# Two interleaved attention and GLU layers on one core: block loads of x, larger stores and head-major loads of block 0, and four attention shifts on TensorE

## The chip, the cores and the metric

The kernel runs on one core of one Trainium2 chip. The metric is the device time of one execution in microseconds (us), the median of several runs. Before the change it is 1635.7 us (three runs, 1635.6 to 1635.84).

## The reference

Two rounds of an attention layer and a gated layer over x of 2048 tokens and 1024 features, all in bf16; each layer works on the layer norm of its input and is added to it.

```python
# attention: 32 heads of 32, window of 8 positions at distance 2 (this token and those 2, 4 .. 14 before it)
qkv = x @ wqkv
idx = pos[:, None] - arange(8) * 2            # masked where negative
logits = einsum("bhsd,bhswd->bhsw", q, k[idx]) * 32 ** -0.5
attn = softmax(logits)
o = einsum("bhsw,bhswd->bhsd", attn, v[idx]) @ wo
# gated layer, F = 3584
h = relu(x @ W_gate) * (x @ W_up)
y = h @ W_down
```

## The kernel before, in words

The 2048 tokens are cut into 4 blocks of 512 tokens (`BLK`), and each block into 4 tiles of 128 (`TPB`). The layers are L = 0 and 2 (attention) and L = 1 and 3 (gated). x stays in SBUF for the whole kernel, in 16 tiles of 128 tokens by 1024 features.

The order on every engine is written out by a small planner, `Plan`. Each piece of work is a step with a due time; `plan.run` sorts the steps by time and issues them in that order, and every engine executes its own steps in the order in which they were issued. `on_pe` hands out TensorE's time group by group (0.216 us a matmul of 512 columns) and so sets the pace. VectorE's attention steps form a chain with ready times, and other VectorE steps are put between them. Weight slabs of 1 MB pass through a ring of five buffers. The due times are only estimates: on the chip each step waits for what it needs, and whatever is behind it on the same engine waits as well.

One attention block goes like this:

- `plan_ln` normalises the block: statistics on ScalarE (an Identity and a Square pass with an accumulator, lines 234 and 235) or on VectorE (`bn`, line 223), 1/sqrt on GpSimd (line 256), the normalised tokens by ScalarE into `xn_all` (line 267; one buffer for all blocks), and two DMA transposes from SP into `xnT` (line 273). Block 0 has its own form in which TensorE transposes.
- `plan_proj` makes q, k and v in the order q, k, v: for each, 8 groups of 8 matmuls (line 391), each group into one of the eight PSUM buffers, evicted by ScalarE (`evict`, line 400) into a staging tile. After every second eviction ScalarE issues a store to the DRAM tensors `q_d`, `k_d` or `v_d` (lines 405 and 408), and GpSimd stores the last 14 tokens of k and v again as the halo of the next block.
- `plan_attn` loads q, k and v back head-major: partition 32·tq + h holds head h of token tile tq, with 32 features by 128 tokens (142 with the halo). Each `piece` (line 519) is a DMA from SP that fills 32 partitions, so there are four for each of q, k and v. On VectorE each of the 8 shifts is a product `pr` (`mul`, line 533) and adds and folds over the 32 features (lines 543, 550, 551); then soft-max with `exp` on ScalarE (line 566), and 8 groups of products with v and their adds (lines 584 to 594). Each group's result goes to `o_d` by a DMA from GpSimd (line 595) and comes back by four DMAs as `oT` (`load_o`, line 603).
- `plan_wo` multiplies by wo: 8 groups of 8 matmuls (line 665) and the residual add on VectorE (line 672), after which the next layer norm begins.

Block 0 of layer 0 is special (`first_logits`). q and k stay in SBUF as `q_fm` and `k_fm`, evicted at line 459 and stored in pairs of chunks at lines 465 and 467. The first `NPE` = 3 of its 8 shifts are done feature-major: VectorE multiplies (`prod`, line 487) and TensorE sums over the features with 32 matmuls into `Lps` (line 497). The other 5 are done head-major after the loads. No other block has shifts on TensorE.

The gated layer is `plan_gu` (gate and up, line 695, `relu` on ScalarE at line 702, product `hT` on VectorE at line 710) and `plan_down` (line 741, add at line 749).

Layer 0 runs over all four blocks first: q, k, v of block 0, of block 1 and so on. The output product of block 0, `wo(0, 0)`, is put inside the projections of block 3 by a hook, here after the third group of k:

```python
hooks = {("k", 0, 2): lambda: wo(0, 0)} if L == 0 and b == NB - 1 else {}
```

The gated layer of block 0 follows v of block 3. The DMAs that SP issues go out in one order: loads of x, slabs, head-major loads, oT loads and transposes. A DMA also waits for an earlier one whose completion semaphore it reuses; there are eight of those for SP and ScalarE together.

Of the kernel before, what the change touches and what calls it, by code (L numbers as in the profile page):

```python
# [9 lines left out]
BF16 = mybir.dt.bfloat16  # L10
# [4 lines left out]
P = 128  # L15
D = 1024
H = 32
DH = 32
W = 8
DIL = 2  # L20
HALO = (W - 1) * DIL
KC = D // P
BLK = 512
TPB = BLK // P
# [3 lines left out]
ROW = HALO + BLK  # L28
# [1 line left out]
DG = 4  # L30
RING = 5
NG = DH // DG
NPE = 3


MM = 0.216
# [1 line left out]
T_LAND = 7.0  # L38
PIECE = 4.5


def _ap(t, off, dims):
    return bass.AP(tensor=t.tensor, offset=t.offset + off, ap=[list(t.ap[0])] + [list(d) for d in dims])


def _dram(t, off, dims):
    return bass.AP(tensor=t.tensor, offset=t.offset + off, ap=[list(d) for d in dims])
# [74 lines left out]
def kernel(  # L122
# [11 lines left out]
    nc = tc.nc  # L134
# [3 lines left out]
    NB = S // BLK  # L138
    NT = S // P
# [3 lines left out]
    x_dram = A_x.flatten_outer_dims()  # L143
# [8 lines left out]
    xpool = ctx.enter_context(tc.tile_pool(name="xres", bufs=1))  # L152
# [16 lines left out]
    q_d = [dram.tile([D, BLK], BF16, name=f"q_d{b}") for b in range(NB)]  # L169
    k_d = [dram.tile([D, ROW], BF16, name=f"k_d{b}") for b in range(NB)]  # L170
    v_d = [dram.tile([D, ROW], BF16, name=f"v_d{b}") for b in range(NB)]
    o_d = [dram.tile([TPB, H, DH, P], BF16, name=f"o_d{b}") for b in range(NB)]
    x_tiles = [xpool.tile([P, D], BF16, name=f"x{t}") for t in range(NT)]

    def consts_early():
        nc.gpsimd.memset(ident[:], 1.0)
# [26 lines left out]
    plan = Plan(RING)  # L203
# [243 lines left out]
    def first_logits(st, tm):  # L447
        hold = {}

        def begin():  # L450
            hold["q"] = tpose.tile([P, KC * BLK], BF16, tag="T", name="q_fm")
            hold["k"] = tpose.tile([P, FRONT + KC * BLK], BF16, tag="T", name="k_fm")
            nc.gpsimd.memset(hold["k"][:, 0:FRONT], 0.0)

        def evict(nm, c, acc, t):
            def f():
                f0 = FRONT if nm == "k" else 0
                fm = hold[nm]
                nc.scalar.copy(fm[:, f0 + c * BLK:f0 + (c + 1) * BLK], acc()[:])
                if c % 2 == 0:  # L460
                    return
                src = fm[:, f0 + (c - 1) * BLK:f0 + (c + 1) * BLK].rearrange("p (c n) -> p c n", c=2)
                r0 = (c - 1) * P
                if nm == "q":
                    nc.scalar.dma_start(_dram(q_d[0], r0 * BLK, [[BLK, P], [P * BLK, 2], [1, BLK]]), src)
                    return
                nc.scalar.dma_start(_dram(k_d[0], r0 * ROW + HALO, [[ROW, P], [P * ROW, 2], [1, BLK]]), src)
                nc.gpsimd.dma_start(_dram(k_d[1], r0 * ROW, [[ROW, P], [P * ROW, 2], [1, HALO]]), src[:, :, BLK - HALO:BLK])
            if nm == "q" and c == 0:
                plan.at(t - 1.0, begin)  # L470
            plan.at(t, f)
            if nm == "k":
                plan.chain.append((lambda: t + 0.7, 1.2, mul(c), None))

        def mul(c):
            def f():
                if c == 0:
                    pr = held[:, 3 * KC:3 * KC + NPE, :]
                elif c == 1:
                    pr = at_pool.tile([P, NPE, BLK], BF16, tag="l1", name="prod_1")  # L480
                else:
                    if c == 2:
                        hold["pr"] = hm_pool.tile([P, 2, NPE, BLK], BF16, tag="v", name="prod_2")
                    elif c % 2 == 0:
                        hold["pr"] = at_pool.tile([P, 2, NPE, BLK], BF16, tag="pr", name=f"prod_{c}", bufs=2)
                    pr = hold["pr"][:, c % 2]
                nc.vector.tensor_tensor(pr[:], _ap(hold["q"], c * BLK, [[0, NPE], [1, BLK]]),
                                        _ap(hold["k"], FRONT + c * BLK, [[-DIL, NPE], [1, BLK]]), op=ALU.mult)
                hold[("pr", c)] = pr
            return f  # L490

        def red():
            L = hold["L"] = psum.tile([P, NPE, P], F32, tag="acc", name="Lps")
            for c in range(KC):
                pr = hold.pop(("pr", c))
                for tq in range(TPB):
                    nc.tensor.matmul(L[32 * tq:32 * tq + 32, :, :], lhsT=wide[:, 28 - 4 * c:60 - 4 * c],
                                     rhs=pr[:, :, tq * P:(tq + 1) * P], start=(c == 0), stop=(c == KC - 1),
                                     skip_group_check=True, tile_position=(0, 32 * tq))

        def out():
            st["L"] = at_pool.tile([P, W, P], F32, tag="L", name="L_0_0")
            nc.scalar.copy(st["L"][:, 0:NPE, :], hold["L"][:])

        def step():
            plan.at(plan.on_pe(8.0, red) + T_EV, out)

        return {"evict": evict, ("v", 0, 3): step}


    def plan_attn(L, b, ends, st, tm):

        def load(t, parts, gap=PIECE):

            def piece(nm, src, row, n, tq):
                def f():
                    if tq == 0:
                        st[nm] = hm_pool.tile([P, DH, n], BF16, tag=nm, name=f"{nm}hm_{L}_{b}")
                    nc.sync.dma_start(st[nm][32 * tq:32 * tq + 32, :, :],
                                      _dram(src[b], tq * P, [[DH * row, H], [row, DH], [1, n]]))  # L520
                return f
            for p in parts:
                for tq in range(TPB):
                    plan.at(t, piece(*p, tq))
                    t += gap
            return t - gap + T_LAND
# [81 lines left out]
        prev = list(chain_tm)  # L608
        chain_tm.append(tm)

        def qk_ready():
            if first:
                load(ends["q"] + 5.5, (("q", q_d, BLK, P),), 1.5)
                tm["qk_in"] = load(ends["k"] + 4.0, (("k", k_d, ROW, HALO + P),), 1.5)
                return tm["qk_in"]
            t = max(ends["k"] + 6.0, prev[-1]["logits"] + 0.5)
            tm["qk_in"] = load(t, (("q", q_d, BLK, P), ("k", k_d, ROW, HALO + P)))
            return tm["qk_in"]

        def v_ready():  # L620
            t = max(ends["v"] + 6.0, tm["qk_in"] + 10.0)
            if prev:
                t = max(t, prev[-1]["pv"] + 0.5)
            return load(t, (("v", v_d, ROW, HALO + P),))

        now = lambda: 0.0
        first = L == 0 and b == 0
# [146 lines left out]
    def proj(L, b):  # L774
        st, tm = {}, {}
        if L == 0 and b == 0:
            hooks = first_logits(st, tm)
        else:
            hooks = {("k", 0, 2): lambda: wo(0, 0)} if L == 0 and b == NB - 1 else {}
        attn[(L, b)] = plan_attn(L, b, plan_proj(L, b, hooks), st, tm)  # L780

    def wo(L, b):
        plan_wo(L, b, attn[(L, b)], plan_ln(L + 1, b))

    def late_ln(L, b, t, on_vector=False):
        for i, f in enumerate(plan_ln(L, b, on_vector=on_vector)):
            f(t + 2.7 * i * (not on_vector))


    def load_x(t, eng=nc.sync):  # L790
        return lambda: eng.dma_start(x_tiles[t][:], x_dram[t * P:(t + 1) * P, :])  # L791
# [16 lines left out]
    for t, at in ((1, -6.7), (2, -6.3), (3, -6.2)):  # L808
        plan.at(at, load_x(t))
    plan.at(14.0, consts_late)  # L810
    for b in range(1, NB):
        for t in range(b * TPB, (b + 1) * TPB):
            plan.at((-4.5, -1.5, 20.5)[b - 1], load_x(t))

    for b in range(NB):
        if b == 0:
            late_ln(0, 1, plan.pe + 7.0, on_vector=True)
            late_ln(0, 2, plan.pe + 30.0)
        elif b == 1:
            late_ln(0, 3, plan.pe + 15.0)  # L820
        proj(0, b)
    for b in range(NB):
        if b >= 1:
            late_ln(2, b - 1, plan.pe + 30.0)
        glu[b] = plan_gu(1, b)
        if b + 1 < NB:
            wo(0, b + 1)
        else:
            wo(2, 0)
        plan_down(1, b, glu[b], False)  # L830
        if b >= 1:
            if b == NB - 1:
                late_ln(2, b, plan.pe + 15.0)
            proj(2, b - 1)
    for b in range(NB):
        glu[b] = plan_gu(3, b)
        if b == 0:
            proj(2, NB - 1)
        if b + 1 < NB:
            wo(2, b + 1)  # L840
        plan_down(3, b, glu[b], True)
# [35 lines left out]
```

## Time and profile before

| | |
|---|---|
| median of three runs | 1635.7 us |
| profiled execution, its own time | 1636.91 us |
| its span, first to last instruction | 1635.2 us |
| TensorE busy | 1617.6 us, 99% of the span |
| VectorE busy | 1045.1 us, 64% |
| ScalarE busy | 448.6 us, 27% |
| GpSimd busy | 102.5 us, 6% |
| mean granted TensorE clock | 0.997 |
| DMA | 319 MB in 456298 packets, mean 195 GB/s |

Times in the profile count from the first instruction of the span. "PE" is TensorE, "PEld" its weight loads, "DVE" VectorE, "ACT" ScalarE, "POOL" GpSimd and "SP" the sync engine, which issues most DMAs; a "q" behind an engine's name is its instruction queue. `xnT<-xn_all` is a DMA or an instruction that writes `xnT` from `xn_all`. The waits of an engine read: who waited at which line, for what, us in total, how often, and the longest.

### The profile page before, as it was taken

How to read it: one execution, taken by the hardware profiler on the slowest of the kernel's cores; microseconds unless marked ns; L12 is line 12 of the kernel's file. 1: busy time of each engine (PE TensorE's matmuls, PEld its weight loads, DVE VectorE, ACT ScalarE, POOL GpSimd, SP SyncE). 2: the span in 40 equal slices, each digit the busy share in tenths (PEclk: the TensorE clock that was granted, in tenths of full speed). 3: DMA queues.
4: the chain of work that ended last, by engine and by line, in shares of the span. 5: the costliest groups of instructions: out<-in, count | busy, mean ns of one | idle time of the engine just before them, and what ended most of it. 6: DMA issues, size and time to landing. Idle time of an engine off the chain costs nothing.

```text
span 1635.2 us, 19283 instructions
## 1 busy us (share of the span) xinstructions
PE 1617.6 (99%) x7658; PEld 741.1 (45%) x7658; DVE 1045.1 (64%) x1297; ACT 448.6 (27%) x718; POOL 102.5 (6%) x170
## 2 busy tenths in 40 slices
PE   9999899999999999999999999999999999999999
PEld 5444344444444444444444444444444444444444
DVE  5399979999999449880598706996999211211211
ACT  4662411303230342403413151133011301121110
POOL 2122000000000100001000010000000000000000
PEclk9999999999999999999999999999999999999999
DMA  9986868778956889568795699599846755565442
GB/s 294 188 212 155 190 162 215 190 192 201 244 168 205 242 192 232 157 212 246 192 228 170 209 228 217 162 265 237 224 149 198 197 176 160 175 173 162 155 164 68
DMA packets 456298, 319.13 MB, mean 195 GB/s; under 512 B 204016, under 2 KB 452240, under 8 KB 456208
## 3 DMA queue, kind: packets, MB, share of 16 engines
q1 hardware_dynamic: 424992, 283.60, 66.1%
q10 hardware_dynamic: 26544, 25.50, 5.3%
q0 software_dynamic: 4672, 8.80, 1.8%
q8 instruction: 60, 0.98, 0.3%
q14 instruction: 30, 0.25, 0.1%
HBM read 263.98 MB, written 38.15 MB: 185 GB/s over the span
## 4 chain that ended last, share of the span: by engine, by line
PE 92%; DMA 3%; DVE 2%; SPq 1%; ACT 1%; issue 0%; ACTq 0%; DVEq 0%
PE acc_g L695 24%; PE acc_u L695 24%; PE dacc L741 24%; PE acc_wo L665 6%; PE acc_k L391 5%; PE acc_q L391 5%; PE acc_v L391 5%; DMA xnT<-xn_all 1%; DVE l L543 1%; SPq L791 1%; DMA x<-in_A_x_dram 1%; DVE pr L533 1%; DMA oT<-o_d 1%; DMA k_d<-stage_k 0%; SPq L198 0%
## 5 line engine op out<-in xcount | busy, mean ns | idle before, releaser
L695 PE MATMUL acc_g<-xnT,wg 128*128 128x512 bf16 x1792 | 425.0, 380 | 6.6 <-DMA xnT<-xn_all 6.6
L695 PE MATMUL acc_u<-xnT,wu 128*128 128x512 bf16 x1792 | 424.5, 380 | 0.0
L741 PE MATMUL dacc<-wd,hT 128*128 128x512 bf16 (+1 forms) x1820 | 388.1, 376 | 0.0
L710 DVE TENSOR_TENSOR hT<-acc_u,r 128x512 bf16<-128x512 f32 x224 | 154.2, 689 | 326.7 <-PE acc_u L695 321.4
L702 ACT ACTIVATE r<-acc_g 128x512 bf16<-128x512 f32 x224 | 133.6, 596 | 710.0 <-PE acc_g L695 710.0
L695 PEld LDWEIGHTS <-wg 128*128 128x128 bf16 x1792 | 175.6, 98 | 219.2 <-issue 8.7
L741 PEld LDWEIGHTS <-hT 128*128 128x128 bf16 x1820 | 178.1, 98 | 209.0
L695 PEld LDWEIGHTS <-wu 128*128 128x128 bf16 x1792 | 175.7, 98 | 212.7 <-issue 2.2
L533 DVE TENSOR_TENSOR pr<-qhm,khm 128x4096 bf16<-128x4096 bf16 x61 | 139.3, 2283 | 24.3 <-DMA khm<-k_d 24.3
L543 DVE TENSOR_TENSOR l<-l,pr 128x1024 f32<-128x1024 f32 x122 | 149.0, 1221 | 2.7
L584 DVE TENSOR_TENSOR pvt<-a,vhm 128x4096 bf16<-128x4096 bf16 x64 | 146.2, 2284 | 0.2
L749 DVE TENSOR_TENSOR x<-dacc,x 128x512 bf16<-128x512 f32 (+1 forms) x65 | 42.9, 680 | 123.4 <-PE dacc L741 123.1
L665 PE MATMUL acc_wo<-wo,oT 128*128 128x512 bf16 x512 | 112.2, 379 | 2.8 <-DMA oT<-o_d 2.8
L391 PE MATMUL acc_v<-xnT,wv 128*128 128x512 bf16 x384 | 84.5, 379 | 0.4 <-ACT stage_k L400 0.3
L391 PE MATMUL acc_q<-xnT,wq 128*128 128x512 bf16 x384 | 84.2, 379 | 0.0
L391 PE MATMUL acc_k<-xnT,wk 128*128 128x512 bf16 x384 | 84.2, 379 | 0.0
L234 ACT ACTIVATE xn_all<-x 128x1024 bf16<-128x1024 bf16 x56 | 59.0, 1053 | 81.4 <-DVE x L672 72.6
L592 DVE TENSOR_TENSOR pvt<-pvt 128x2048 bf16<-128x2048 bf16 x64 | 78.1, 1221 | 1.4
L665 PEld LDWEIGHTS <-oT 128*128 128x128 bf16 x512 | 49.8, 98 | 64.0 <-DMA oT<-o_d 4.3
L267 ACT ACTIVATE xn_all<-x,nb,rstd 128x1024 bf16<-128x1024 bf16 x60 | 72.0, 1234 | 18.9 <-DVE nb L261 15.1
L595 POOL DMA_DIRECT2D o_d<-ohm x64 | 35.3, 552 | 644.3 <-DVE ohm L594 630.7
L543 DVE TENSOR_TENSOR l<-pr 128x1024 f32<-128x1024 bf16 x61 | 74.3, 1218 | 0.8
(84 smaller groups left out, 826.2 us busy)
## 6 DMA issues: line engine op xcount, KB each, us to landing
wg<-in_B_W_gate_dram SPq DMA_DIRECT2D x56, 1024.0 KB, 7.0
wu<-in_B_W_up_dram SPq DMA_DIRECT2D x56, 1024.0 KB, 5.3
wd<-in_B_W_down_dram SPq DMA_DIRECT2D x48, 1024.0 KB, 6.4
wo<-in_A_wo_dram SPq DMA_DIRECT2D x16, 1024.0 KB, 7.0
wq<-in_A_wqkv_dram SPq DMA_DIRECT2D x9, 1024.0 KB, 4.9
wk<-in_A_wqkv_dram SPq DMA_DIRECT2D x9, 1024.0 KB, 5.5
wv<-in_A_wqkv_dram SPq DMA_DIRECT2D x9, 1024.0 KB, 6.0
khm<-k_d SPq DMA_DIRECT2D x32, 284.0 KB, 8.8
```

The lines of the kernel that those rows point to most:

```text
L234: nc.scalar.activation(junk, xt[:], ACT.Identity, accum_out=st[:, 0, t % 2:t % 2 + 1])
L267: nc.scalar.activation(hold["xn"][:, t, :], x_tiles[b * TPB + t][:], ACT.Identity, scale=rstd[:, i:i + 1], bias=nb[:, i:i + 1])
L391: nc.tensor.matmul(acc[:, t0 * P:t1 * P], lhsT=w["t"][:, kc, j * P:(j + 1) * P], rhs=xnT[(L, b)][:, t0:t1, kc, :], start=(kc == 0), stop=( ...
L533: nc.vector.tensor_tensor(pr[:], st["q"][:], _ap(st["k"], HALO - DIL * w, [[HALO + P, DH], [1, P]]), op=ALU.mult)
L543: nc.vector.tensor_tensor(l[:], pr[:, 0:8] if i == 0 else l[:], pr[:, 8 * i + 8:8 * i + 16], op=ALU.add)
L584: nc.vector.tensor_tensor(tt[:], a_bc, v_sh, op=ALU.mult)
L592: nc.vector.tensor_tensor(tt[:, 0:4], tt[:, 0:4], tt[:, 4:8], op=ALU.add)
L665: nc.tensor.matmul(acc[:], lhsT=st["oT"][:, c, t, :], rhs=ws[half]["t"][:, c, :], start=(c == 0), stop=(c == KC - 1))
L695: nc.tensor.matmul(acc[:], lhsT=w["t"][:, kc, (j % 4) * P:(j % 4 + 1) * P], rhs=xnT[(L, b)][:, :, kc, :], start=(kc == 0), stop=(kc == KC ...
L702: nc.scalar.activation(r[:], hold.pop(("g", j))[:], ACT.Relu)
L710: nc.vector.tensor_tensor(st["hT"][:, j, :], hold.pop(("u", j))[:], hold.pop(("r", j))[:], op=ALU.mult)
L741: nc.tensor.matmul(accs[(t, c0)][:], lhsT=st["hT"][:, j, t * P:(t + 1) * P], rhs=w["t"][:, jl, c0 - half * SLAB:c0 - half * SLAB + n], sta ...
```

## The change

It has these parts:

- `NPE` goes from 3 to 4: block 0 of layer 0 has four shifts on TensorE and four on VectorE.
- x is held in one tile a block. Blocks 1, 2 and 3 are loaded by one DMA of 1 MB each, not four of 256 KB; the due time of block 3's load goes from 20.5 to 50.0.
- The stores of `q_fm` take four chunks each (two DMAs, not four); those of `k_fm` take four, two and two (three DMAs).
- The head-major loads of q and k of block 0 of layer 0 take two token tiles each (`m=2`), so two DMAs of 64 partitions stand in place of four of 32, and its v loads are due 2.5 apart.
- The head-major loads of v of block 1 of layer 0 are due after the `oT` loads of block 0.
- The statistics of block 2 of layer 0 are computed on VectorE (`bn`), due at 32 in place of 30 after the start of block 0's projections; those of block 3 are due at 20 in place of 15.
- `wo(0, 0)` is put after the last group of q of block 3, three groups of k sooner.

```diff
-NPE = 3
+NPE = 4
...
-    x_tiles = [xpool.tile([P, D], BF16, name=f"x{t}") for t in range(NT)]
+    x_blk = [xpool.tile([P, TPB, D], BF16, name=f"xb{b}") for b in range(NB)]
+    x_tiles = [x_blk[t // TPB][:, t % TPB, :] for t in range(NT)]
...
-                if c % 2 == 0:
+                n = {3: 4, 5: 2 * (nm == "k"), 7: 2 if nm == "k" else 4}.get(c, 0)
+                if n == 0:
                     return
-                src = fm[:, f0 + (c - 1) * BLK:f0 + (c + 1) * BLK].rearrange("p (c n) -> p c n", c=2)
-                r0 = (c - 1) * P
+                src = fm[:, f0 + (c + 1 - n) * BLK:f0 + (c + 1) * BLK].rearrange("p (c n) -> p c n", c=n)
+                r0 = (c + 1 - n) * P
...
-        def load(t, parts, gap=PIECE):
+        def load(t, parts, gap=PIECE, m=1):
...
-                    nc.sync.dma_start(st[nm][32 * tq:32 * tq + 32, :, :],
-                                      _dram(src[b], tq * P, [[DH * row, H], [row, DH], [1, n]]))
+                    dims = [[DH * row, H], [row, DH], [1, n]]
+                    nc.sync.dma_start(st[nm][32 * tq:32 * (tq + m), :, :],
+                                      _dram(src[b], tq * P, dims if m == 1 else [[P, m]] + dims))
                 return f
             for p in parts:
-                for tq in range(TPB):
+                for tq in range(0, TPB, m):
...
-                load(ends["q"] + 5.5, (("q", q_d, BLK, P),), 1.5)
-                tm["qk_in"] = load(ends["k"] + 4.0, (("k", k_d, ROW, HALO + P),), 1.5)
+                load(ends["q"] + 5.5, (("q", q_d, BLK, P),), 2.0, 2)
+                tm["qk_in"] = load(ends["k"] + 4.0, (("k", k_d, ROW, HALO + P),), 2.0, 2)
...
-            if prev:
-                t = max(t, prev[-1]["pv"] + 0.5)
+            if first:
+                return load(t, (("v", v_d, ROW, HALO + P),), 2.5)
+            t = max(t, prev[-1]["done"] - T_LAND + 1.0 if b == 1 and L == 0 else prev[-1]["pv"] + 0.5)
...
-            hooks = {("k", 0, 2): lambda: wo(0, 0)} if L == 0 and b == NB - 1 else {}
+            hooks = {("q", 1, 3): lambda: wo(0, 0)} if L == 0 and b == NB - 1 else {}
...
-    for b in range(1, NB):
-        for t in range(b * TPB, (b + 1) * TPB):
-            plan.at((-4.5, -1.5, 20.5)[b - 1], load_x(t))
+    for b, at in ((1, -4.5), (2, -1.5), (3, 50.0)):
+        plan.at(at, lambda b=b: nc.sync.dma_start(x_blk[b][:], _dram(x_dram, b * BLK * D, [[D, P], [P * D, TPB], [1, D]])))
...
-            late_ln(0, 2, plan.pe + 30.0)
+            late_ln(0, 2, plan.pe + 32.0, on_vector=True)
         elif b == 1:
-            late_ln(0, 3, plan.pe + 15.0)
+            late_ln(0, 3, plan.pe + 20.0)
```

In the head-major loads the source pattern of a 32-partition load is (rows one `row` apart, 1024 of them; n tokens each); that of a 64-partition load is (2 token tiles, 128 tokens apart; 1024 rows; n tokens). The destinations are 32 and 64 partitions.

More of the change, by code (lines that the diff above doesn't have):

```diff
@@ L459, in f @@
                 nc.scalar.copy(fm[:, f0 + c * BLK:f0 + (c + 1) * BLK], acc()[:])
-                if c % 2 == 0:
+                n = {3: 4, 5: 2 * (nm == "k"), 7: 2 if nm == "k" else 4}.get(c, 0)
+                if n == 0:
                     return
-                src = fm[:, f0 + (c - 1) * BLK:f0 + (c + 1) * BLK].rearrange("p (c n) -> p c n", c=2)
-                r0 = (c - 1) * P
+                src = fm[:, f0 + (c + 1 - n) * BLK:f0 + (c + 1) * BLK].rearrange("p (c n) -> p c n", c=n)
+                r0 = (c + 1 - n) * P
                 if nm == "q":
-                    nc.scalar.dma_start(_dram(q_d[0], r0 * BLK, [[BLK, P], [P * BLK, 2], [1, BLK]]), src)
+                    nc.scalar.dma_start(_dram(q_d[0], r0 * BLK, [[BLK, P], [P * BLK, n], [1, BLK]]), src)
                     return
-                nc.scalar.dma_start(_dram(k_d[0], r0 * ROW + HALO, [[ROW, P], [P * ROW, 2], [1, BLK]]), src)
-                nc.gpsimd.dma_start(_dram(k_d[1], r0 * ROW, [[ROW, P], [P * ROW, 2], [1, HALO]]), src[:, :, BLK - HALO:BLK])
+                nc.scalar.dma_start(_dram(k_d[0], r0 * ROW + HALO, [[ROW, P], [P * ROW, n], [1, BLK]]), src)
+                nc.gpsimd.dma_start(_dram(k_d[1], r0 * ROW, [[ROW, P], [P * ROW, n], [1, HALO]]), src[:, :, BLK - HALO:BLK])
             if nm == "q" and c == 0:
```

## The prediction

> **What bounds the kernel now.** I read the page's busy line first, then the windows by stage, TensorE's waits, the chain, and the DMA part. From the page:
>
> ```profile
> PE 1617.6 (99%) x7658; PEld 741.1 (45%) x7658; DVE 1045.1 (64%) x1297; ACT 448.6 (27%) x718; POOL 102.5 (6%) x170
> ```
>
> TensorE sets the time; only what it loses can be won. The windows (start and end, PE busy, PEld, DVE, ACT, POOL, granted clock, DMA share, GB/s) show where it loses:
>
> ```profile
> 80.00:90.00 10.00, 8.96 (x41) 3.80 (x39) 9.72 (x11) 9.03 (x18) 1.45 (x2) 1.00 1.19 287
> 90.00:100.00 10.00, 9.38 (x42) 4.00 (x41) 9.48 (x19) 7.37 (x12) 3.99 (x4) 1.00 0.90 168
> 100.00:110.00 10.00, 9.24 (x43) 4.12 (x43) 9.62 (x13) 4.78 (x8) 2.90 (x4) 1.00 0.85 198
> 160.00:170.00 10.00, 8.54 (x40) 3.74 (x39) 9.76 (x11) 0.41 (x1) 0.00 (x0) 1.00 1.22 244
> 170.00:180.00 10.00, 8.69 (x41) 3.73 (x39) 9.93 (x14) 6.13 (x11) 0.00 (x0) 1.00 0.75 159
> 200.00:210.00 10.00, 4.03 (x10) 1.46 (x11) 6.72 (x7) 1.50 (x3) 0.00 (x0) 0.58 0.97 241
> 210.00:220.00 10.00, 10.00 (x43) 4.31 (x42) 6.98 (x8) 1.37 (x3) 0.00 (x0) 0.91 0.00 0
> ```
>
> Three places, all in layer 0. TensorE's waits name them:
>
> ```profile
> PE acc_g L695 <- DMA xnT<-xn_all: 6.6, 1, 6.6
> PE acc_wo L665 <- DMA oT<-o_d: 2.8, 2, 1.5
> PE acc_v L391 <- ACT stage_k L400: 1.1, 2, 0.8
> PE acc_q L391 <- ACT stage_v L400: 1.0, 2, 0.7
> ```
>
> and the chain (start, duration, what) shows where each begins:
>
> ```profile
> 34.95 9.09 DMA xnT<-xn_all
> 60.54 2.27 DMA v_d<-stage_v
> 63.41 5.19 DMA khm<-k_d
> 68.77 2.31 DVE pr L533
> ...
> 113.16 13.81 PE acc_k L391 x64
> ...
> 164.88 8.38 DMA oT<-o_d
> 173.31 3.63 PE acc_wo L665 x16
> ...
> 192.50 13.34 DMA xnT<-xn_all
> 205.97 3.57 PE acc_g L695 x8
> ```
>
> A projection of one block takes TensorE 13.81 us. In the timeline k, v and q of blocks 1 and 2 run from 68.03 to 113.00, 44.97 for 3 × 13.81 = 41.43: 3.5 lost. wo of block 0 runs 159.84 to 176.77, 16.93 for 13.81: 3.1. The gate matmuls start at 205.97, though v of block 3 ended at 199.2: 6.8; the clock is then granted at 0.58 and their first 16 take 6.31 for 3.45: 2.9. Together 16.3 us. All hang on VectorE's pass over block 0, which starts only at 68.77, when the last head-major k load lands.
>
> **The change part by part.** Sums stand against the profiled execution's own 1636.9 us (span 1635.2), 1.2 above the median of 1635.7.
>
> *Four shifts on TensorE.* The 32 Lps matmuls ran 45.75 to 47.30 at 384 columns; at 512 they take 4/3 of 1.55: +0.5. VectorE loses one of block 0's five shifts in the first layer, 7.49 (pr 2.28, three adds of 1.22, folds 1.15 and 0.29, less overlap); no other block has shifts on TensorE. The products grow by a third (0.96 to 1.28 each), done before its loads land.
>
> *Stores, loads of x, statistics.* Of k's four stores the third could be issued only at 44.12, when the transposes of block 1 had landed (44.04), and the evictions behind it stood. Fewer, larger q and k stores take away that wait; k's last store goes out near 39.6 instead of 45.63 and lands, at the same 6.4 us, near 46. Block 3's four x loads (issued 39.19 to 41.18) leave their place ahead of the q loads for one behind block 2's transposes; the first q load then issues near 39.2, not 41.28. Nothing reads that x before 72. Block 2's statistics leave ScalarE (four pairs of 2.36) for VectorE (eight of 0.68), which idles from 44 to 68; cost nothing, and if that cover is gone, 5.4 us of VectorE. With them off ScalarE, its 6.57 us wait for the xn_all buffer (72.7 to 79.25), which made the stage_k and stage_v rows above, comes later and with slack.
>
> *wo of block 0 three groups sooner.* It comes 3 × 8 × 0.216 = 5.2 us nearer to the oT loads; good only if VectorE is at least that much earlier. The v loads of block 1 now queue on SP behind the oT loads and no longer among them (oT landings were 159.79, 164.87, 165.70 and 173.26), and both transposes after wo are issued before the 1 MB wu slab that stood between them (issues 188.69, 190.68 and 192.50).
>
> *The head-major loads of block 0* are what I could not price from one row. Two q and two k loads replace four and four; each fills 64 partitions in 64 × 32 = 2048 pieces of 256 or 284 bytes. The piece price is in the trace: two k loads of 1024 pieces issued at 121.43 and 122.01 landed at 126.39 and 127.68, 1.29 us apart, which is 1024/16 = 64 pieces on each of 16 DMA engines and so 20.2 ns a piece. The page's mean is the dear end:
>
> ```profile
> q1 hardware_dynamic: 424992, 283.60, 66.1%
> ```
>
> 1635.2 × 16 × 0.661 / 424992 = 40.7 ns. What the trace cannot show is over how many engines the new form runs. Every transfer before has 32 or more as its outermost count on both sides (a 32-partition load reads 1024 rows one step apart). The new source is [2, 1024, n], the 2 being the pair of token tiles, a step that joins no other. One end: 16 engines, as the nearest rows. Other end: transfers are dealt out by their outermost count, and 2 engines carry 1024 pieces each. I take 2: the outermost count is the one thing in which the form leaves all rows that show 16, and the transfer is addressed in that order. As the four loads are alike, I put them on the same pair.
>
> The Trainium skill has a rule for it: "DMA: Bandwidth & Descriptors", section "Why a DMA increments its semaphore by 16 and not by 1", says that the engines used are the largest number up to 16 dividing the slowest non-unit dimension of both patterns, and for this issuing path the lowest-numbered ones; its "Rules for kernel authors" warn of an outermost dimension under 16. By it all four loads share one pair of engines; the same page's advice to coalesce into larger transfers would give the 16-engine sum. No run so far shows either.
>
> *The sum with 16 engines.* k loads issue near 46; the first pair of 284 KB takes 4.5 + 1.3, the second 2.6 more: VectorE starts near 55, 14 earlier. Four shifts and soft-max (46.8 before, less 7.49: 39.3), and pv (8 × 4.65): block 0 is done near 131.5, not 152.7. oT lands near 150 for a wo at 151.5; the adds end near 174, the transposes land 188 to 191 for gate matmuls at 193. All 16.3 goes, less 0.5: 1636.9 − 15.8 = 1621.1, at the median 1619.9.
>
> *The sum with one pair.* First pieces move 1.3 us after the issue at 39.2, at 40.5. Four loads in line: 4 × 1024 × 20.2 ns = 82.7, so the last lands near 124 and VectorE starts 69 later than with 16. Behind them on the same two engines lie the shares of block 2's transposes and block 3's x. ScalarE's statistics of block 3 stand in the middle of k of block 1's evictions and wait for both; the eight PSUM buffers fill and TensorE stops near 86 until about 130. It then runs 13.8 us to the third group of q of block 2 (at 99.7 undisturbed), whose buffer needs an eviction queued behind exp of block 0. exp starts four shifts and the maxima after VectorE's start, 124 + 4 × 7.49 + 3.8 = 157.8; exp, one normalisation and one eviction (1.06 + 1.24 + 0.57) free the buffer at about 161. TensorE is 161 − 99.7 = 61 late. The stop before it is inside this 61. Restart at the low clock: 2.9. Later wo, adds and transposes hang on VectorE, now 69 late against TensorE's 64, and the slack there is 2 to 4: 1.5 more. 1621.1 + 61.3 + 2.9 + 1.5 = 1686.8, at the median 1685.6.
>
> Bounds: at 40.7 ns the loads take 166.7 and the end is 84 later, 1770; half way (30.4 ns) 1728. If q and k loads fell on different pairs, k would land at 47.3 + 41.4 = 88.7 and the time would be 1650.
>
> **The rivals.** (1) *Loads at full width.* For: all 96 head-major loads before run at some 20 ns over 16 engines, and the bytes are the same. Against: no row with so small an outermost count. Time 1620, faster by 16. It decides from the point where VectorE starts block 0 by 63: then exp frees the buffer before 99.7. (2) *Full width, but the transposes after wo are late again:* four loads of oT and two 512 KB transposes meet slabs of 1 MB; if the second lands 5 us after 193, 5 + 2.9 come back: 1628. (3) *The loads fall on two pairs:* 1650.
>
> **How the numbers follow.** One pair 0.62, two pairs or something between 0.08, full width 0.30 (of which late transposes 0.06). The likeliest gives the predicted 1686; its own range is 1664 (15 ns a piece, an estimate a quarter under the row) to 1735 (30.4 ns and some waits more). As cases of both signs hold most of the chance, the range runs from 1617 to 1735: full width is in it, and what is left out is the dearest part of the pair case. A measurement of this kernel tells about 0.2% (3.3 us) from no change. Faster takes full width, 0.29; within 0.2% 0.01, a late wo that eats just the gain; slower 0.70.
>
> **What would show it.** Right: khm loads of block 0 landing past 100 with first pr after them; DMA share low while they run (2 of 16 engines busy is 0.12 plus the rest); TensorE idle tens of us between 80 and 165, waiting for ScalarE evictions behind statistics of block 3 and exp; a clock below 1 after it; block 1 and later unchanged in shape. Full width: k loads land by 56, first pr near 55, no PE idle at 80 to 110, none or little at wo and at the first gate matmuls. Wrong altogether: VectorE starting early and TensorE still losing time at wo, or a stop where neither sum has one, as at block 2's transposes with all loads landed.

## The result, and the profile after

The changed kernel takes 1688.9 us (median of four, 1688.3 to 1694.8) against 1635.8: 3.3% slower, ratio 1.0332 (95% interval 1.0309 to 1.0355). The prediction said 1686. The profiled execution took 1688.66, its span 1686.9.

The windows after (columns as before):

```profile
80.00:90.00 10.00, 7.99 (x38) 3.50 (x36) 0.00 (x0) 0.00 (x0) 0.00 (x0) 1.00 0.16 30
90.00:100.00 10.00, 0.00 (x0) 0.00 (x0) 0.00 (x0) 0.00 (x0) 0.00 (x0) 0.56 0.17 26
...
140.00:150.00 10.00, 9.35 (x32) 3.73 (x32) 9.72 (x10) 8.53 (x18) 1.45 (x2) 0.71 1.24 261
150.00:160.00 10.00, 3.71 (x18) 1.57 (x16) 9.55 (x15) 1.35 (x3) 1.06 (x2) 0.80 0.38 116
160.00:170.00 10.00, 7.59 (x26) 2.85 (x26) 8.62 (x18) 8.00 (x10) 2.82 (x4) 0.69 0.45 99
```

From 88 to 129 TensorE, VectorE, ScalarE and GpSimd all stand, and from 90 to 120 the DMA engines move some 30 GB/s. The waits of the engines name the chain:

```profile
DVE pr L536 <- DMA khm<-k_d: 95.9, 3, 80.6
...
ACT xn_all L235 <- DMA xb<-in_A_x_dram: 63.0, 1, 63.0
PE acc_v L392 <- ACT stage_k L401: 52.7, 1, 52.7
...
ACT xn_all L268 <- DVE nb L262: 24.2, 14, 8.9
...
PE acc_q L392 <- ACT stage_v L401: 8.7, 2, 8.3
```

VectorE waits 80.6 us for the head-major k loads; ScalarE 63.0 for block 3's x, which is behind those loads on SP; TensorE 52.7 for the evictions behind ScalarE's wait, and 8.3 more later. The chain (start, duration, what) starts the first `pr` at 129.49 where it was 68.77:

```profile
86.44 42.85 DMA khm<-k_d
129.49 2.30 DVE pr L536
```

SP's own timeline shows the four loads:

```profile
42.41 24.55 SPq L522 DMA_DIRECT2D qhm<-q_d  x2
67.15 40.75 SPq L522 DMA_DIRECT2D khm<-k_d  x2
108.02 23.16 SPq L274 DMA_TRANSPOSE xnT<-xn_all  x2
131.23 0.99 SPq L816 DMA_DIRECT2D xb<-in_A_x_dram  x1
```

Before, eight such issues took from 41.28 to 64.07, 0.5 to 2.4 us each. Now the issues end at 43.06, 66.96, 86.39 and 107.90 and the first transpose's at 129.12: SP can go on only once in about 20 us. The DMA view of 90 to 120 has nothing but these pieces in it:

```profile
DMA packets 2972, 0.84 MB, mean 28 GB/s; under 512 B 2972, under 2 KB 2972, under 8 KB 2972
q1 hardware_dynamic: 2972, 0.84, 16.9%
```

If two engines carry them, 2972 pieces in 30 us are 30000 × 2 / 2972 = 20.2 ns a piece and engine, the price that the prediction took from two k loads of the kernel before.

### The profile page after: what moved, and what is told of

Read it like the earlier page. It is cut to its first block, busy times and chain, and to the rows that moved or that the text cites. A ratio compares the mean times of both kernels' runs of the same rounds, so it can differ in the third digit from the quotient of the medians.

```text
span 1686.9 us, 19239 instructions
## 1 busy us (share of the span) xinstructions
PE 1618.1 (96%) x7658; PEld 741.4 (44%) x7658; DVE 1043.9 (62%) x1296; ACT 441.1 (26%) x702; POOL 102.7 (6%) x169
## 4 chain that ended last, share of the span: by engine, by line
PE 86%; DVE 7%; DMA 4%; issue 2%; SPq 0%; POOL 0%; ACT 0%; ACTq 0%; DVEq 0%; POOLq 0%
PE acc_g L699 23%; PE acc_u L699 23%; PE dacc L745 23%; PE acc_wo L669 6%; PE acc_k L392 4%; PE acc_q L392 4%; PE acc_v L392 4%; DMA khm<-k_d 3%; DVE l L546 2%; DVE pr L536 1%; DVE pvt L587 1%; DVE l L553 1%; DVE pvt L595 1%; DMA xnT<-xn_all 0%; SPq L522 0%
## 5 line engine op out<-in xcount | busy, mean ns | idle before, releaser
L753 DVE TENSOR_TENSOR xb<-dacc,xb 128x512 bf16<-128x512 f32 (+1 forms) x65 | 43.3, 681 | 124.4 <-PE dacc L745 124.2
L235 ACT ACTIVATE xn_all<-xb 128x1024 bf16<-128x1024 bf16 x52 | 54.8, 1053 | 136.3 <-DVE xb L676 70.9
L392 PEld LDWEIGHTS <-wqk 128*128 128x128 bf16 x480 | 42.7, 99 | 107.9 <-issue 67.6
L392 PE MATMUL acc_v<-xnT,wqk 128*128 128x512 bf16 x128 | 30.1, 394 | 52.7 <-ACT stage_k L401 52.7
L268 ACT ACTIVATE xn_all<-xb,nb,rstd 128x1024 bf16<-128x1024 bf16 x60 | 71.9, 1233 | 26.9 <-DVE nb L262 24.2
L401 ACT CAST stage_q<-acc_q 128x512 bf16<-128x512 f32 x56 | 32.2, 586 | 170.5 <-PE acc_q L392 162.0
```

What stands on the lines that cost most here:

```text
L235: nc.scalar.activation(junk, xt[:], ACT.Identity, accum_out=st[:, 0, t % 2:t % 2 + 1])
L268: nc.scalar.activation(hold["xn"][:, t, :], x_tiles[b * TPB + t][:], ACT.Identity, scale=rstd[:, i:i + 1], bias=nb[:, i:i + 1])
L392: nc.tensor.matmul(acc[:, t0 * P:t1 * P], lhsT=w["t"][:, kc, j * P:(j + 1) * P], rhs=xnT[(L, b)][:, t0:t1, kc, :], start=(kc == 0), stop=( ...
```

## The experiments

All were timed beside the kernel before on the same chip; its median there was 1637.4 (for the first four runs), 1635.6 (m1_npe3, m1_pairs, head_major_store, m1_stats) and 1635.5 us (the rest). Ratios are to it, with 95% intervals.

**Which property of the loads costs**

*after_m1*: the loads alone put back.

```diff
-                load(ends["q"] + 5.5, (("q", q_d, BLK, P),), 2.0, 2)
-                tm["qk_in"] = load(ends["k"] + 4.0, (("k", k_d, ROW, HALO + P),), 2.0, 2)
+                load(ends["q"] + 5.5, (("q", q_d, BLK, P),), 2.0 / 3)
+                tm["qk_in"] = load(ends["k"] + 4.0, (("k", k_d, ROW, HALO + P),), 2.0 / 3)
```

> The changed kernel with only the head-major q and k loads of block 0 put back to eight DMAs of 32 partitions (outermost count 1024), in the same places. Theory, the four loads ran on two of the 16 engines and that is the whole loss: the last k load lands near 55, the first pr starts near 56 and not 129.5, TensorE loses under 1 us between 80 and 215, and the time is 1619.9 (within 3). Rival, other parts of the change cost as well (a transpose or a wo that is late again): 1625 to 1640. Rival, the loads had nothing to do with it: 1689.

1629.1, ratio 0.9950 (0.9937 to 0.9964); profiled 1629.55. The loads are the loss, but the time is over the stated 1619.9 (within 3): the rest brings 8 us and not 16, as the first rival said. The last k load landed at 65.9 and the first `pr` started at 66.05, not near 56. TensorE's waits:

```profile
PE acc_q L392 <- ACT stage_v L401: 3.1, 3, 2.1
PE acc_k L392 <- DVE xb L676: 3.0, 1, 3.0
PE acc_g L699 <- DMA xnT<-xn_all: 1.8, 1, 1.8
```

*after_rows*: the same 64 partitions and 2048 pieces, another outermost count (the new line is for `m == 2` alone).

```diff
-                                      _dram(src[b], tq * P, dims if m == 1 else [[P, m]] + dims))
+                                          _dram(src[b], min(tq * P, row // 2 - n), [[row // 2, 2 * D], [1, n]]))
```

> The changed kernel with its four loads of 64 partitions and 2048 pieces kept, but each reads 2048 half rows one step apart, so that the outermost count is 2048 and not 2. The pieces have the same size and number; the data are other parts of q and k, so the attention of block 0 in layer 0 is another. Theory, the outermost count alone decides: first pr near 56, 1620 (within 3), like eight loads of 32 partitions. Rival, a DMA of 64 partitions or 2048 pieces is itself slow: first pr near 129 and 1689.

1625.6, ratio 0.9928 (0.9914 to 0.9941), profiled 1623.70; first `pr` at 64.11. That is like after_m1, and not the stated 1620 (within 3). The size of the load is not what costs; in SP's timeline the four issues are short again:

```profile
39.33 8.65 SPq L523 DMA_DIRECT2D qhm<-q_d  x2
52.29 4.83 SPq L523 DMA_DIRECT2D khm<-k_d  x2
```

*after_m4*: one load of 128 partitions for q and one for k.

```diff
-                load(ends["q"] + 5.5, (("q", q_d, BLK, P),), 2.0, 2)
+                load(ends["q"] + 5.5, (("q", q_d, BLK, P),), 2.0, 4)
```

(and k alike)

> The changed kernel with one q and one k load of 128 partitions each, outermost count 4. Theory, as many engines as the outermost count: 2 x 4096 pieces on 4 engines is 2048 each, at 20.9 ns 43 us; the first load issues near 42.4, pieces move from 43.7, the first pr starts near 87, and the third group of q of block 2 gets its buffer near 124 for 99.7: 24 late, restart 2.9, and 1 to 2 later, 1648 in all (1642 to 1654). Rival, two engines whatever the count: 1689. Rival, a larger DMA is quicker: 1620.

1656.8, ratio 1.0120 (1.0105 to 1.0134), profiled 1653.5: between the two, where only "as many engines as the outermost count" puts it, though above the stated 1642 to 1654. First `pr` at 91.70, not 87. TensorE waited 30.6 in place of 24, and not where expected: the wait ends at 95.86, in q of block 1. On ScalarE block 2's normalisation stood ahead of the last evictions of block 0's v and waited for `nb`, which VectorE computed right after the first `pr`:

```profile
94.09 1.24 ACT L268 ACTIVATE xn_all<-xb,nb,rstd 128x1024 bf16<-128x1024 bf16 x1 [41.82 <-DVE nb L262]
```

The DMA view of 70 to 88:

```profile
q1 hardware_dynamic: 3267, 0.93, 33.3%
```

That is twice the share of the loads with a count of 2. On four engines it is 18000 × 4 / 3267 = 22.0 ns a piece.

*before_m2*: the kernel before with only the new loads.

```diff
-                load(ends["q"] + 5.5, (("q", q_d, BLK, P),), 1.5)
+                load(ends["q"] + 5.5, (("q", q_d, BLK, P),), 2.0, 2)
```

(k alike, and `load` and `piece` as in the change)

> The kernel before with only the four loads of 64 partitions (outermost count 2) in place of eight of 32. Theory, this part alone makes the loss: the first q load issues near 41.3, pieces move for 4096 x 20.9 ns = 86 us, the first pr starts near 129 and not 68.8, 60 later; TensorE is later by that less the few us of slack in front of exp: 1690 to 1698. Rival, the loss needs the other parts (moved stores, statistics, wo): under 1680.

1688.3, ratio 1.0314 (1.0300 to 1.0328), 2 under the stated range; first `pr` at 126.44. This one part makes all of the loss; on top of it the rest of the change brings nothing that shows. Here too the stop is not the one in front of `exp`: ScalarE waited 58.6 for `nb`, again behind the first `pr`, and TensorE 56.8 for the evictions behind it.

```profile
ACT xn_all L267 <- DVE nb L261: 77.9, 15, 58.6
...
PE acc_q L391 <- ACT stage_v L400: 62.1, 2, 56.8
```

**Where the other half of the gain went: one part of after_m1 undone at a time**

*m1_npe3*, `-NPE = 4` `+NPE = 3`:

> after_m1 with three shifts on TensorE again. Theory, VectorE's pass over block 0 sets the end of the loss: one shift more is 7.5 us later at exp, wo and the gate matmuls, less 0.5 for Lps and less whatever wait is covered: 5 to 9 slower than after_m1. Rival, the slack covers it: the time of after_m1 within 1.

Ratio 0.9941 (0.9927 to 0.9954): nothing is lost, and the theory fell. One shift more on VectorE, after a first `pr` that is 1.1 later, makes soft-max of block 0 8.7 us later (first `pvt` at 113.96 for 105.26). But the planner then puts the wo adds behind two shifts of block 1 and not three, and they start at 166.13 instead of 170.89.

*m1_pairs*:

```diff
-                n = {3: 4, 5: 2 * (nm == "k"), 7: 2 if nm == "k" else 4}.get(c, 0)
+                n = 2 * (c % 2)
```

> after_m1 with the q_fm and k_fm stores in pairs of chunks again. In after_m1 the second q store took 16 us to land (27.2 to 43.2), and the q loads waited for it. Theory A (the prediction's): pairs bring the third k store's wait for the transposes back, k lands 3 to 6 later: 2 to 6 slower than after_m1. Theory B, the larger stores gain nothing here, as the q loads wait for the last q store: within 2 of after_m1, or faster.

Ratio 0.9950 (0.9938 to 0.9963): theory B in the time, though not in its reason. The last q store landed sooner than in after_m1, at 40.7 for 43.2, but the q loads then waited until 43.3 for the transposes of block 1. The last k store lands at 53.4 instead of 49.8, but the first `pr` moves only from 66.05 to 66.90.

*head_major_store*: q and k stores write the order of the head-major loads.

```diff
-                    nc.scalar.dma_start(_dram(q_d[0], r0 * BLK, [[BLK, P], [P * BLK, n], [1, BLK]]), src)
+                    nc.scalar.dma_start(_dram(q_e, r0 * TPB * P, [[P, P], [P * P, n * TPB], [1, P]]),
+                                        _ap(fm, (c + 1 - n) * BLK, [[P, n * TPB], [1, P]]))
...
+                        nc.sync.dma_start(st[nm][32 * tq:32 * tq + 32, :, :].rearrange("p d n -> p (d n)"),
+                                          _dram(src, tq * P * n, [[TPB * P * n, KC], [DH * n, 4], [1, DH * n]]))
```

> after_m1 with the stores of q and k of block 0 writing DRAM in the order the head-major loads want: the stores have pieces of 256 and 284 bytes (2048 in one of four chunks), the eight loads 32 pieces of 8 or 9 KB each (outermost counts 8 and 32). In after_m1 the eight loads were issued over 43.2 to 60.6 and landed 52.3 to 65.9. Theory A, these loads then land one fast after the other, the last near 56, first pr near 56 and not 66; the 10 us take out the waits at wo and the gate matmuls: 5 to 8 less than after_m1. Theory B, the small pieces only move to the stores, whose landings slip by as much: first pr 63 to 66 and the time of after_m1 within 2.

Ratio 0.9952 (0.9939 to 0.9964): theory B in the time. The last two k stores landed at 57.9 and 59.0, not 49.8, and the first `pr` started at 69.06, later than both theories said.

*m1_stats*:

```diff
-            late_ln(0, 2, plan.pe + 32.0, on_vector=True)
+            late_ln(0, 2, plan.pe + 30.0)
-            late_ln(0, 3, plan.pe + 20.0)
+            late_ln(0, 3, plan.pe + 15.0)
```

> after_m1 with block 2's statistics on ScalarE again (due 30) and block 3's due at 15. Theory (the prediction's), ScalarE's wait for the xn_all buffer returns in the middle of k and v of block 1, and with it some 3.5 us of TensorE between 80 and 110, part of which the later waits would have cost anyway: 1 to 4 slower than after_m1. Rival, with VectorE's start at 66 the end of the layer is set by VectorE alone: within 1.

Ratio 0.9970 (0.9959 to 0.9982), 3 us slower than after_m1. The size was as expected, the place was not: TensorE's largest wait is 4.8 for the wo adds.

*m1_x*: x by tiles, block 3's at 20.5.

```diff
-    for b, at in ((1, -4.5), (2, -1.5), (3, 50.0)):
-        plan.at(at, lambda b=b: nc.sync.dma_start(x_blk[b][:], ...
+    for b in range(1, NB):
+        for t in range(b * TPB, (b + 1) * TPB):
+            plan.at((-4.5, -1.5, 20.5)[b - 1], load_x(t))
```

> after_m1 with x of blocks 1 to 3 loaded by tiles again, block 3's at the old due time, ahead of the q loads. Prediction's theory, the four loads ahead of q delay it by 2 us and so the first pr: 1 to 3 slower than after_m1. Rival, the q loads wait for the q store anyway (43.2): within 1.

Ratio 0.9965 (0.9952 to 0.9977), 2.5 us slower, with the first `pr` at 69.81, 3.8 later. Block 3's four loads do stand at 43.52 to 45.52 ahead of the q loads. But the trace shows a second delay: ScalarE's second k store waited until 41.03 for the second q store to land, and the last one was issued at 48.87, for 39.43 in after_m1. What each of the two costs was not measured apart.

*m1_wo*, the hook `("q", 1, 3)` back to `("k", 0, 2)`:

> after_m1 with wo of block 0 back three groups later (after the third group of k). Theory, its 5.2 us are only a place: the adds on VectorE, behind three shifts of block 1, and the transposes after them set the gate matmuls, so TensorE's 3.0 at the wo adds goes and the wait at the gate matmuls grows by as much: within 1.5 of after_m1. Rival, the sooner wo makes its stall: 2 to 3 faster.

Ratio 1.0008 (0.9999 to 1.0017): all of after_m1's gain is gone, against both expectations. The adds end 3.6 us later (185.0 for 181.3), and the gate matmuls start at 206.59, for 201.23. The profile puts their wait to v's evictions on ScalarE:

```profile
PE acc_g L699 <- ACT stage_v L401: 8.4, 1, 8.4
```

But the last of these evictions ended at 205.89, and the second transpose behind the adds landed only at 206.5 (issued at 195.34, 11.2 to land). On SP a 1 MB wu slab stands between the two transposes again, as in the kernel before:

```profile
192.20 1.90 SPq L274 DMA_TRANSPOSE xnT<-xn_all  x1
194.21 1.00 SPq L199 DMA_DIRECT2D wu<-in_B_W_up_dram  x1
195.34 6.36 SPq L274 DMA_TRANSPOSE xnT<-xn_all  x1
```

In after_m1 both transposes (from 183.66 and 193.5) are ahead of that slab (195.37). So the wait ends with the transpose; the evictions alone would have ended it 0.7 sooner.

**Order or speed**

In after_m1 `exp` of block 0 is ahead of six of v's evictions, and the wo adds are behind three shifts. Its ScalarE timeline from 99.8, and then VectorE's from 161 (start, duration, engine, line, operation; idle time before it and what ended it in brackets):

```profile
99.82 1.06 ACT L569 ACTIVATE L<-L 128x1024 f32<-128x1024 f32 x1 [1.28 <-DVE L L566]
100.79 1.23 ACT L268 ACTIVATE xn_all<-xb,nb,rstd 128x1024 bf16<-128x1024 bf16 x1
101.92 0.56 ACT L401 CAST stage_v<-acc_v 128x512 bf16<-128x512 f32 x1
```

```profile
161.19 2.29 DVE L536 TENSOR_TENSOR pr<-qhm,khm 128x4096 bf16<-128x4096 bf16 x1
...
168.69 2.28 DVE L536 TENSOR_TENSOR pr<-qhm,khm 128x4096 bf16<-128x4096 bf16 x1
170.89 1.28 DVE L676 TENSOR_TENSOR xb<-acc_wo,xb 128x512 bf16<-128x512 f32 x2
```

*m1_due8* tells the planner a later landing, nothing else:

```diff
-                tm["qk_in"] = load(ends["k"] + 4.0, (("k", k_d, ROW, HALO + P),), 2.0 / 3)
+                tm["qk_in"] = load(ends["k"] + 4.0, (("k", k_d, ROW, HALO + P),), 2.0 / 3) + 8.0
```

> after_m1 with one number changed: the planner takes the k loads of block 0 to land 8 us later than it did (it had put them some 14 us before the 66 at which the first pr starts). Nothing is added or removed; the orders change: exp of block 0 comes behind more evictions of v of block 1 on ScalarE, and the adds of wo of block 0 come behind two and not three shifts of block 1 on VectorE. Theory, what is left of the loss in after_m1 is order, not speed: TensorE's waits for ScalarE stage_v (3.1), for the wo adds (3.0) and at the gate matmuls (1.8) go, 5 to 8 faster than after_m1. Rival, VectorE's start itself is the limit: the waits only move, within 2.

1621.4, ratio 0.9916 (0.9902 to 0.9929), some 6 us under after_m1 as expected and the fastest here: 0.8% under the kernel before and 4% under the changed one. The first `pr` still starts at 64.86. TensorE loses nothing in these windows any more:

```profile
100.00:110.00 10.00, 10.00 (x48) 4.53 (x47) 7.78 (x9) 5.49 (x10) 1.45 (x2) 1.00 1.10 224
...
170.00:180.00 10.00, 10.00 (x48) 4.49 (x46) 9.65 (x18) 8.24 (x14) 2.24 (x2) 1.00 0.47 138
...
200.00:210.00 10.00, 10.00 (x48) 4.51 (x46) 9.83 (x12) 1.79 (x3) 0.00 (x0) 1.00 0.41 124
```

VectorE's timeline shows the adds behind two shifts of block 1, from 160.25:

```profile
152.76 2.29 DVE L536 TENSOR_TENSOR pr<-qhm,khm 128x4096 bf16<-128x4096 bf16 x1
...
160.25 0.68 DVE L676 TENSOR_TENSOR xb<-acc_wo,xb 128x512 bf16<-128x512 f32 x1
```

*m1_due8_x*: block 2's x due at 26.0 in place of -1.5.

> m1_due8 with block 2's x loaded behind block 1's transposes and not ahead of them. Theory, the DMA engines are full from 20 to 50 (their shares are over 1), and 1 MB less before the transposes lets these, the q store and the k stores land 2 to 4 earlier: first pr 62 to 64; the time is that of m1_due8 or up to 3 less. Rival, the x then lands too late for block 2's statistics on VectorE, which stand ahead of the first pr: first pr 66 or later, and nothing gained.

Ratio 0.9936 (0.9924 to 0.9949), 3 us slower than m1_due8. The first `pr` came at 63.93, as the theory said, but the time did not follow. The last q store did land 5 earlier and the last k store 1 to 2, but the x landed at 57.05 and block 2's transposes were issued at 65.3 and 72.2, not 63.3 and 65.4. TensorE waited 3.6 for ScalarE's evictions of v.

## Why the prediction was right, and where it was not

**The engines** (the open step): the end that the prediction took, two engines, was met, and so was the price inside it, 20.2 ns. Outermost counts of 2, 4 and 1024 or more in the source start VectorE at 129.5, 91.7 and 64 to 66. In pieces a us, the two k loads of the kernel before gave 1024 / 1.29 = 794; a count of 2 gave 2972 / 30 = 99, an eighth of that, and a count of 4 gave 3267 / 18 = 182, a little under a quarter. That agrees with the rule of the Trainium skill in "DMA: Bandwidth & Descriptors", section "Why a DMA increments its semaphore by 16 and not by 1", which no row before showed. No view here shows single engines. That the loads went one after the other, with SP let on at 66.96, 86.39 and 107.90, fits the rule's lowest-numbered engines, and two pairs would not do it. The same page's advice on disjoint partition halves, "Don't bother", is not tested by itself: after_rows, with halves at full width, starts VectorE 2 us before after_m1 with its quarters, but its q loads also went out 3.9 sooner (39.33 for 43.24).

**The start.** The first q load was issued at 42.41, not 39.2: the second transpose of block 1 kept SP until 40.42, and the load then waited 1.9 for the last q store. With 42.41 + 1.3 + 82.7 the loads would end at 126.4; the first `pr` came at 129.49, 5.5 later than said.

**The stops.** Said: one stop from 86 to about 130 and another until 161, 61 in all. Measured: 88.0 to 140.65 (52.7) and 153.7 to 162.03 (8.3), with 0.4 after it 61.4. The first was longer than said since SP, held by the loads, issued the second transpose and block 3's x only at 129 to 132. The second stop is in front of the second group of q of block 2, and not of the third: block 3's first normalisation waited 8.9 for `nb`, which VectorE computes behind its fourth shift (ScalarE works again at 160.26). The third group then waited another 0.4, and this wait is the one that the prediction named: `exp`, one normalisation and one eviction. TensorE's timeline, and then ScalarE's:

```profile
162.03 3.57 PE L392 MATMUL acc_q<-xnT,wqk 128*128 128x512 bf16 x8 [8.32 <-ACT stage_v L401]
165.97 3.76 PE L392 MATMUL acc_q<-xnT,wqk 128*128 128x512 bf16 x16 [0.37 <-ACT stage_v L401]
```

```profile
163.26 1.06 ACT L569 ACTIVATE L<-L 128x1024 f32<-128x1024 f32 x1 [1.29 <-DVE L L566]
164.23 1.23 ACT L268 ACTIVATE xn_all<-xb,nb,rstd 128x1024 bf16<-128x1024 bf16 x1
165.36 0.56 ACT L401 CAST stage_v<-acc_v 128x512 bf16<-128x512 f32 x1
```

The third group started at 165.97 and not at 161, as the first `pr` was 5.5 later than said.

**After the stops.** Against m1_due8, which has no stop, wo of block 0 starts 218.09 − 151.29 = 66.8 later and the gate matmuls 260.48 − 192.74 = 67.7: 61.4 of stops, 0.4 from before them, about 5 after the two stops (said 2.9, for one restart; the clock is at 0.71, 0.80 and 0.69 in the three windows above), and 0.9 (said 1.5) at the gate. The spans differ by 1686.9 − 1619.3 = 67.6; the two sums of the prediction by 65.7. That they come so close is in part luck. At the third group TensorE is 66.5 late (165.97 for 99.5 in m1_due8, where q starts at 96.04 and a group takes 1.73), 5 more than the 61.3 said. The slow clock fell almost all ahead of that group, inside this delay: up to wo only 0.3 came on top, and not 2.9.

**The rival at full width** was priced at 1621.1 of own time. Loads of 64 partitions at full width took 1623.70 (after_rows, profiled), and the eight loads of 32 partitions 1629.55 (after_m1), so that sum was 2.6 to 8.4 short. The mis-sized term is the landing of the stores. The sum put k's last store at 6.4 us, and it took 11.4 in after_rows, where the k loads wait for it, and 10.4 in after_m1 (39.43 to 49.8). In after_m1 the path runs through the second q store, which took 16.1 (27.17 to 43.23; the last q store before took 7.5), and on through the loads:

```profile
27.17 16.05 DMA q_d<-q_fm
...
43.96 9.60 DMA qhm<-q_d
...
53.72 6.36 DMA khm<-k_d
60.09 5.84 DMA khm<-k_d
...
66.05 2.30 DVE pr L536
```

The windows of the kernel before and of the changed one have DMA shares over 1 from 10 to 50 us. The same q store took 6.1 (m1_due8_x) to 17.2 (m1_npe3) over the runs, and the last pair of q chunks in m1_pairs took 13.0: the larger stores did not land sooner. So VectorE starts at 64 to 66 and not at 55. But the same 1621.1 is reached by m1_due8 (profiled 1621.06) with VectorE at 64.9: what the 10 us cost was not VectorE's work but the instruction orders, made for loads that land sooner than they do. That four shifts and larger stores were worth something here is not borne out (m1_npe3, m1_pairs). The sooner wo is the part with the largest effect (m1_wo). The prediction called it "good only if VectorE is at least that much earlier", by 5.2 us. In after_m1 it is: block 0's pass over v ends at 142.1, for 152.4 before. But in m1_npe3 the pass ends at 150.8, only 1.6 sooner, and the sooner wo still cost TensorE no more than 2.2 us of waiting for `oT`, so the "only" is too strong.

The shares of the parts do not add up, as each undone part also moves other steps in the planner's order. How much each would bring with the orders of m1_due8 was not measured.

## What to carry to other kernels

Look at the outermost count of a DMA's pattern before joining two into one (the source's was the one varied here): a load twice as large whose source starts with a 2 moved its pieces at the rate of two engines, took some 20 us instead of a few, and held everything behind it on its queue. Where orders are written out from estimated times, measure the landing after each change of loads and put it into the estimate: one number was worth 5 to 6 us here, where the change without its loads had brought 8. And price a landing from rows at the same DMA load, not from the quiet ones.

## What the runs showed of the hardware

The issuing queue is held as well: SP's second q load took 23.8 us to issue (43.12 to 66.96), the k loads 19.2 and 21.5, and the next transpose 21.1, where a 32-partition load before took 0.5 to 2.4. So the transposes and block 3's x, which were issued behind the loads, waited for them as well. And a DMA share is not a count of engines: the loads whose rate is that of two engines of 16 read 0.169 and not 0.125, those at the rate of four 0.333 and not 0.25.
